# Decode attention: PV with V as the moving operand in four column tiles, the diagonal taken out by masked sums and one fp32 matmul

## The chip, the cores and the metric

The kernel runs on one core of one Trainium2 chip. The metric is the device time of one execution in microseconds. Inputs lie in HBM; the core has five engines with a queue of instructions each: TensorE (PE, with its weight loads as PEld), VectorE (DVE), ScalarE (ACT), GpSimd (POOL) and SyncE (SP), which here issues all DMAs.

## The reference

Two layers of grouped-query decode attention, each followed by a small dense block, for 8 sequences of one token. Every layer reads the same K and V caches: 8 sequences x 8 kv heads x 8192 keys x 128, bf16, K and V 134 MB each. Four query heads share one kv head.

```python
def _A_ref(x, k_cache, v_cache, wq, wo):          # x (8, 1, 512)
    q = (x @ wq).reshape(B, 1, 32, 128).transpose(0, 2, 1, 3)
    k, v = jnp.repeat(k_cache, 4, axis=1), jnp.repeat(v_cache, 4, axis=1)
    scores = jnp.einsum("bhqd,bhkd->bhqk", q, k) * 128 ** -0.5
    o = jnp.einsum("bhqk,bhkd->bhqd", softmax(scores), v)
    return o.transpose(0, 2, 1, 3).reshape(B, 1, 4096) @ wo
def _B_ref(x, w1, w2):                             # 512 -> 1792 -> 512
    return silu(x @ w1) @ w2

x = x + _A_ref(_layernorm(x), k_cache, v_cache, wq, wo)
x = x + _B_ref(_layernorm(x), w1, w2)
x = x + _A_ref(_layernorm(x), k_cache, v_cache, wq, wo)
x = x + _B_ref(_layernorm(x), w1, w2)
```

## The kernel before

**Tasks, positions, granules.** One task is one (layer, sequence, kv head): 128 tasks. A task has 8 positions of 1024 keys (8 chunks of 128); two positions are one granule of 2048 keys, which is one tile of 512 KB of K or V in one slot of the arena (`NSLOT` = 27 slots). `make_tasks` orders the tasks so that the two layers interleave: the transposed K of the last five kv heads of a sequence (20 granules, `KEEP`) stays in the arena from layer 0 to layer 1. So 88 tasks load K and V and transpose K; 40 tasks (layer 1, kept heads) load V only and need no transposes. `plan_loads` sorts all loads by the position that needs them and gives each the slot that comes free first; `issue_until(p)` at the end of each position issues, on SP's queue, the loads whose slot has been given up by then. A DMA waits on the queue for the instructions that still read its slot.

**One loop over positions** (L744) writes all engines' work in order; each engine runs its queue in that order. `op` and `mm_group` put a semaphore wait in front of an instruction where a resource that it reads or writes was last touched by another engine (or by VectorE or ScalarE themselves). At position p the loop does, in this order:
- at p7 (p mod 8 = 7), the four query columns of the next task go into `QB` (ScalarE, L452);
- `emit_t`: 8 transposes of the K chunks into a PSUM bank `TPp` (L429, three banks), then one copy back into the arena over the same chunks: the granule's first half (even p) on ScalarE (L435), the second (odd p) on VectorE (L437);
- at odd p, `emit_pv` twice (L533): the PV matmuls of the granule 12 positions back (`LP`);
- a piece of the softmax of the task before, by p mod 8 (`soft`): p0 row maximum and `spread` (L471, L473); p1 the shift: an fp32 matmul with `ones` (L481), `own`, `shift` (L484, L487) and the exponential on ScalarE (L491), which writes P; p3 the sums (L497, and a reduction over partitions on GpSimd, L500); p4 four transposes of P and the copy to `PT` (L509, L513); p7 the reciprocal;
- if a layer chain is pending, its next stage; else, at some odd p, a group of 16 output-projection matmuls (`add_heads`, L627);
- at odd p, `emit_s` (L460): the scores of the granule, 4 matmuls that stream 512 keys each past 32 query columns into four column tiles of one PSUM bank. They need both halves' copies;
- at p4, for the task whose PV ended at p3, `emit_norm` (L547) on VectorE.

**Scores.** The four column tiles take the four quarters of a granule; granule k of the task shifts the query columns by k within the tile, so that after four granules the bank holds 4 tiles x (4 query heads x 4 granules) rows of 512 scores. After the transposes of P, `PT` holds for each key lane the weights by chunk x (0 to 3 within a quarter), quarter c, head r and granule k.

**PV.** Each of the 64 chunks of V (128 keys x 128) is the stationary operand, and its four weight columns, each repeated 12 times (`PVN`), are the moving one; all 64 matmuls accumulate into one PSUM region of the bank `OTp`, 128 x 48, of which every twelfth column is used. The same bank is also the target of the shift matmul.

**Layer chains.** When the last task of a sequence in layer 0 is normed, a chain of stages follows, one per position: the remaining `add_heads`, the residual, the layer norm (`first` to `fourth`, short VectorE operations with two reductions on GpSimd), the dense block in two pieces each (28 matmuls a piece), `silu`, a layer norm again, and the query projection of layer 1 in 8 pieces. There are eight such chains. The final dense block for all sequences stands at the end.

Of the kernel before, what the change touches and what calls it, by code (L numbers as in the profile page):

```python
# [29 lines left out]
FAR = 1e38  # L30
PVN = 12
CW = 32
# [176 lines left out]
def _build(ctx, nc, A_x, A_k_cache, A_v_cache, A_wq, A_wo, B_w1, B_w2, out):  # L209
# [58 lines left out]
    QT2 = [sb([128, HQ], BF16, "QT2") for _ in range(2)]  # L268
    QB = [sb([128, NGRAN - 1 + QUAD], BF16, "QB") for _ in range(NQB)]
    at1 = [sb([128, HQ], BF16, "at1") for _ in range(3)]  # L270
    at2 = sb([128, HQ, B], BF16, "at2")
    vr = sb([128, B], FP32, "vr")
# [11 lines left out]
    Xr = P  # L284
    PT = [sb([128, CPB, NQ * USED], BF16, "PT") for _ in range(NPT)]
    ones = sb([128, 128], FP32, "ones")
    hm = sb([128, REP], FP32, "hm")
    real = sb([128, 1], FP32, "real")
    far = sb([128, NQ * USED], FP32, "far")
    rowmax = sb([128, 1], FP32, "rowmax")  # L290
# [25 lines left out]
    def r_half(slot, h):  # L316
        return res(f"slot{slot}_{h}")
# [40 lines left out]
    with nc.Block() as block:  # L358

        @block.sync  # L360
        def _(sync_eng):
# [12 lines left out]
            for n in range(NQB):  # L374
# [4 lines left out]
                lambda: dve.tensor_reduce(  # L379
                    hm[:, :], lanes.rearrange("p c (r k) -> p r c k", k=NGRAN), AX.XY, ALU.add),  # L380
                reads=["ident"], writes=["hm"],
            )
            op(dve, lambda: dve.tensor_reduce(real[:, :], hm[:, :], AX.X, ALU.add), reads=["hm"], writes=["real"])
            for c in range(NQ):
                op(dve, lambda c=c: dve.tensor_scalar(
                    far[:, c * USED:(c + 1) * USED].rearrange("p (r k) -> p r k", k=NGRAN),
                    hm[:, :].unsqueeze(2).to_broadcast([128, REP, NGRAN]), real[:, 0:1], -FAR,
                    op0=ALU.subtract, op1=ALU.mult),
                   reads=["hm", "real"], writes=["far"])
# [21 lines left out]
            evacs = [0]  # L411
            tnext = [0]

            def has_t(i):
# [7 lines left out]
            def emit_t(i):  # L422
                b, g, k, h = where(i)
                slot = k_slot[(b, g, k)]
                tb = evacs[0] % NTP
                evacs[0] += 1
                tpv = TPp[tb][:, :].rearrange("p (k q) -> p k q", q=128)
                steps = [
                    lambda c=c: pe.transpose(tpv[:, c, :], chunk(slot, h * GRP + c), ident[:, :])  # L429
                    for c in range(GRP)  # L430
                ]
                mm_group(steps, reads=[r_half(slot, h), "ident"], writes=[f"TP{tb}"])
                dst = half(slot, h)
                if h == 0:
                    op(act, lambda: act.copy(dst, TPp[tb][:, :]), reads=[f"TP{tb}"], writes=[r_half(slot, h)])  # L435
                else:
                    op(dve, lambda: dve.tensor_copy(dst, TPp[tb][:, :]), reads=[f"TP{tb}"], writes=[r_half(slot, h)])  # L437
# [7 lines left out]
            def emit_q(ti):  # L445
                layer, b, g = tasks[ti]
                if layer == 0:
                    q, rq = QT1[:, b * HQ + g * REP:b * HQ + (g + 1) * REP], "QT1"
                else:
                    q, rq = QT2[b % 2][:, g * REP:(g + 1) * REP], f"QT2_{b % 2}"  # L450
                qb = QB[ti % NQB][:, NGRAN - 1:NGRAN - 1 + USED].rearrange("p (r k) -> p r k", k=NGRAN)[:, :, 0]
                op(act, lambda: act.copy(qb, q), reads=[rq], writes=[f"QB{ti % NQB}"])  # L452

            def emit_s(i):
                ti = i // GPT
                b, g, k, _h = where(i)
                slot = k_slot[(b, g, k)]
                bank, qn = ti % NSCP, ti % NQB
                steps = [
                    lambda c=c: pe.matmul(  # L460
                        SCp[bank][c * QUAD:(c + 1) * QUAD, :], QB[qn][:, NGRAN - 1 - k:NGRAN - 1 - k + QUAD],
                        ARENA[:, slot * SLOT + c * KB:slot * SLOT + (c + 1) * KB],
                        start=(k == 0), stop=(k == NGRAN - 1),
                    )
                    for c in range(NQ)
                ]
                mm_group(steps, reads=[r_half(slot, 0), r_half(slot, 1), f"QB{qn}"], writes=[f"SC{bank}"])

# [34 lines left out]
            def emit_pt(ti):  # L503
# [9 lines left out]
                op(dve, lambda: dve.tensor_copy(  # L513
                    PT[pb][:, :, :].rearrange("p x (c q) -> p x c q", q=USED),
                    tpv.rearrange("p x (c q) -> p x c q", q=QUAD)[:, :, :, 0:USED]),
                   reads=[f"TP{tb}"], writes=[f"PT{pb}"])

# [4 lines left out]
            def emit_pv(i):  # L522
                ti = i // GPT
                b, g, k, h = where(i)
                slot = v_slot[(b, g, k)]
                ob, pb = ti % 2, ti % NPT
                pv = PT[pb][:, :, :].rearrange("p x (c r k) -> p x c k r", c=NQ, k=NGRAN)
                otp = OTp[ob][:, 0:REP * PVN].rearrange("p (r n) -> p r n", n=PVN)
                steps = []
                for c in range(GRP):  # L530
                    cc = (i % GPT) * GRP + c
                    steps.append(
                        lambda c=c, cc=cc: pe.matmul(  # L533
                            otp, chunk(slot, h * GRP + c), pv[:, cc % CPB, cc // CPB % NQ, k, :].unsqueeze(2).to_broadcast([128, REP, PVN]),
                            start=(cc == 0), stop=(cc == NCH - 1),
                        )
                    )
                mm_group(steps, reads=[r_half(slot, h), f"PT{pb}"], writes=[f"OT{ob}"])

            def emit_norm(ti):  # L540
# [4 lines left out]
                else:  # L545
                    dst, rd = at2[:, g * REP:(g + 1) * REP, b], "at2"
                op(dve, lambda: dve.tensor_tensor(dst, OTp[ob][:, 0:REP * PVN:PVN], rcp[st][:, :], ALU.mult),  # L547
                   reads=[f"OT{ob}", f"rcp{st}"], writes=[rd])
# [72 lines left out]
            def wo_part(g, rhs_of, r_rhs, n, first, last):  # L621
                w = CW if n == 1 else n
                steps = []
                for o in range(KT):
                    for h in range(g * REP, (g + 1) * REP):
# [7 lines left out]
                        )  # L633
                mm_group(steps, reads=["wo", r_rhs], writes=["MISC"])

# [51 lines left out]
            def query(n, dst_of, rdst, parts=1):  # L687
# [4 lines left out]
                        lambda: dve.tensor_copy(dst_of, MISC[:, 0:HQ * n].rearrange("p (h b) -> p h b", b=n)),  # L692
                        reads=["MISC"], writes=[rdst],
                    ))

            def chain_of(b):
                xs = [XT[n][:, :, b:b + 1] for n in range(3)]
                st = block_stages(xs, ["XT0", "XT1", "XT2"], 1, True)
                st += ln_stages(xs[2], "XT2", 1) + settle
                return st + query(1, QT2[b % 2][:, 0:HQ].rearrange("p (h b) -> p h b", b=1), f"QT2_{b % 2}", QPARTS)  # L700

# [3 lines left out]
            def add_heads(b):  # L705
# [3 lines left out]
                if b < B:  # L709
                    a = at1[b % 3]  # L710
                    wo_part(g, lambda h: a[:, h:h + 1], f"at1_{b % 3}", 1, first, last)
                else:
                    wo_part(g, lambda h: at2[:, h, :], "at2", B, first, last)

# [16 lines left out]
            soft = {0: [softmax_max], 1: [softmax_shift, softmax_exp], 3: [softmax_sum], 4: [emit_pt], 7: [softmax_rcp]}  # L731
            for f in query(B, QT1[:, 0:B * HQ].rearrange("p (b h) -> p h b", h=HQ), "QT1"):
                f()

            emit_q(0)

            chain = []
            chain_b = [None]
# [4 lines left out]

            for p in range(NG + LP + GPT + 1):  # L744
                tq = (p + LQ) // GPT
# [6 lines left out]
                emit_t_until(p + LT)  # L752
                if p % GPG == GPG - 1:
                    for i in range(p - LP - GPG + 1, p - LP + 1):
                        if 0 <= i < NG:
                            emit_pv(i)
                ti, ph = p // GPT - 1, p % GPT
# [3 lines left out]
                if chain:  # L761
                    left = max(1, first1[chain_b[0]] - EARLY - p)
                    late = len(chain) <= QPARTS or len(chain) > left + QPARTS // 2
                    for _n in range(2 if late and len(chain) > left else 1):
                        chain.pop(0)()
                elif heads[turn[0]] and (p >= NG or turn[0] == B
                                         or p % GPG == GPG - 1 and (tasks[p // GPT][2], 0) in kept):
                    add_heads(turn[0])
                if p < NG and p % GPG == GPG - 1:
                    emit_s(p)  # L770
                done = p - LP - GPT
                if done >= 0 and done % GPT == 0 and done // GPT < ntask:
                    tj = done // GPT
                    emit_norm(tj)
                    layer, b, _g = tasks[tj]
                    if layer == 0:
                        heads[b].append(_g)
                    elif b == B - 1:
                        heads[B].append(_g)
                    if layer == 0 and tj == last0[b]:  # L780
                        assert not chain and turn[0] == b
# [52 lines left out]
```

## Time and profile before

| | |
|---|---|
| median of 3 runs | 1204.68 us (1202.18 to 1208.07) |
| profiled execution, its own time | 1209.39 us |
| profiled execution, span from the first to the last instruction | 1207.3 us |
| mean granted TensorE clock | 0.974 |
| HBM read | 465.05 MB |
| DMA rate in the slices of the span | 355 to 410 GB/s, the first and last slices aside |
| busy: PE, PEld, VectorE, ScalarE, GpSimd | 977, 777, 564, 463, 71 us |
| K copies: ScalarE (352), VectorE (352) | 1010 ns, 692 ns each |
| PV matmuls | 8192 |
| score matmuls | 2048 |
| chain that ended last, by engine | PE 50%, DMA 19%, DVE 18%, SP's queue 5%, issue 5%, ACT 3% |

Busy time is the union of an engine's instructions, matmul ends are modelled, and a busy TensorE includes waiting in its pipeline. A timeline row gives the start in us from the span's start, the duration in us, the engine, the line of the kernel, the operation, what it writes and reads, the number of instructions merged in it, and, in brackets, the idle time of the engine before it with the instruction that ended it. A row of a group in the page ends with its busy time, the mean ns of one and the idle time before.

### The profile page before, as it was taken

What the parts mean: (1) busy time and instruction counts of PE and PEld (TensorE: products, weight loads), DVE (VectorE), ACT (ScalarE), POOL (GpSimd) and SP (SyncE); (2) the same over time, 40 slices, a digit from 0 to 9 for tenths busy, and PEclk for the clock granted to TensorE, in tenths of its full rate; (3) what the DMA queues carried; (4) which work ended last, traced back from release to release, by engine and by line L of the source; (5) the groups of instructions that cost most, each with busy time, mean ns of one, the idle gap of its engine ahead of it and who ended that gap; (6) DMA issues with size and microseconds to landing.
All of it is one profiled execution on the core that took longest, in us unless ns stands there. A gap on an engine that the chain in (4) does not pass through costs nothing.

```text
span 1207.3 us, 45534 instructions
## 1 busy us (share of the span) xinstructions
PE 976.7 (81%) x19960; PEld 777.3 (64%) x19960; DVE 563.8 (47%) x1745; ACT 462.5 (38%) x746; POOL 70.9 (6%) x172
## 2 busy tenths in 40 slices
PE   3688887888888888888888888888788888888785
PEld 3566675766667675676666765667576766677564
DVE  2434453545344553455344544445344543445443
ACT  1334341544235431453244432544144422454241
POOL 0000000000000000000000000000000000000000
PEclk9989998999899998999999999999999997999997
DMA  9999999999999999999999999999999999999993
GB/s 370 385 397 407 394 358 403 408 399 385 387 408 407 401 367 409 408 394 388 379 408 406 399 365 408 408 405 362 398 408 406 393 371 409 408 366 377 393 407 155
DMA packets 131622, 468.03 MB, mean 388 GB/s; under 512 B 13904, under 2 KB 19808, under 8 KB 130912
## 3 DMA queue, kind: packets, MB, share of 16 engines
q1 hardware_dynamic: 131424, 465.12, 98.6%
q8 instruction: 158, 2.59, 0.9%
q14 instruction: 40, 0.33, 0.1%
HBM read 465.05 MB, written 0.01 MB: 385 GB/s over the span
## 4 chain that ended last, share of the span: by engine, by line
PE 50%; DMA 19%; DVE 18%; SPq 5%; issue 5%; ACT 3%; POOL 0%; POOLq 0%; ACTq 0%; DVEq 0%
PE TPp L429 19%; PE SCp L460 11%; DVE arena L437 9%; DMA arena<-in_A_v_cache_dram 9%; PE OTp L533 9%; DMA arena<-in_A_k_cache_dram 8%; SPq L333 5%; PE MISC L609 4%; PE TPp L509 3%; DVE rowmax L471 2%; DMA wo<-in_A_wo_dram 2%; PE OTp L481 2%; ACT P L491 2%; PE MISC L627 2%; DVE PT L513 1%
## 5 line engine op out<-in xcount | busy, mean ns | idle before, releaser
L435 ACT COPY arena<-TPp 128x1024 bf16<-128x1024 bf16 x352 | 355.7, 1010 | 437.2 <-PE TPp L429 437.1
L429 PE MATMUL TPp<-ident,arena 128*128 128x128 bf16 x5632 | 403.3, 222 | 25.0 <-DMA arena<-in_A_k_cache_dram 11.0
L429 PEld LDWEIGHTS TPp<-ident,arena 128*128 128x128 bf16 x5632 | 325.3, 99 | 111.3 <-issue 73.2
L437 DVE COPY arena<-TPp 128x1024 bf16<-128x1024 bf16 x352 | 243.3, 692 | 263.0 <-PE TPp L429 256.6
L533 PE MATMUL OTp<-PT,arena 128*128 128x48 bf16 x8192 | 299.8, 185 | 45.4 <-DVE at L547 17.6
L533 PEld LDWEIGHTS OTp<-PT,arena 128*128 128x128 bf16 x8192 | 256.6, 97 | 106.6 <-issue 77.7
L460 PE MATMUL SCp<-arena,QB 128*32 128x512 bf16 x2048 | 211.5, 401 | 97.3 <-DVE ssm L497 32.4
L491 ACT ACTIVATE P<-SCp,shift 128x512 bf16<-128x512 f32 x128 | 88.0, 687 | 279.9 <-PE OTp L533 163.0
L471 DVE TENSOR_REDUCE rowmax<-SCp 128x1 f32<-128x512 f32 x128 | 88.5, 692 | 129.5 <-PE SCp L460 129.5
L460 PEld LDWEIGHTS SCp<-arena,QB 128*32 128x32 bf16 x2048 | 60.3, 94 | 131.4 <-ACT arena L435 45.6
L500 POOL PARTITION_ALL_REDUCE ssa<-ssm x128 | 55.9, 437 | 957.6 <-DVE ssm L497 929.8
L513 DVE COPY PT<-TPp 128x256 bf16<-128x256 bf16 x128 | 37.3, 292 | 112.6 <-PE TPp L509 112.6
L481 PE MATMUL OTp<-spread,ones 128*128 128x64 f32 x256 | 54.6, 295 | 23.6 <-DVE spread L473 22.2
L509 PE MATMUL TPp<-ident,P 128*128 128x128 bf16 x512 | 50.4, 221 | 11.6 <-ACT P L491 11.6
L481 PEld LDWEIGHTS OTp<-spread,ones 128*128 128x128 f32 x256 | 38.7, 191 | 26.8 <-DVE spread L473 26.8
L484 DVE SCALAR_TENSOR_TENSOR own<-OTp,real,far 128x64 f32<-128x64 f32 x128 | 36.3, 284 | 40.3 <-PE OTp L481 40.0
L509 PEld LDWEIGHTS TPp<-ident,P 128*128 128x128 bf16 x512 | 32.6, 98 | 23.5 <-ACT P L491 22.1
L497 DVE TENSOR_SCALAR ssm<-hm,rs 128x4 f32<-128x4 f32 x128 | 28.6, 223 | 36.7 <-ACT P L491 36.7
L627 PE MATMUL MISC<-at,wo 128*128 128x32 bf16 (+1 forms) x1152 | 40.0, 176 | 6.1 <-DMA wo<-in_A_wo_dram 5.9
L609 PE MATMUL MISC<-xnT,wq 128*128 128x32 bf16 (+1 forms) x1152 | 38.7, 176 | 1.9 <-issue 1.9
L627 PEld LDWEIGHTS MISC<-at,wo 128*128 128x128 bf16 x1152 | 35.2, 97 | 6.4 <-DMA wo<-in_A_wo_dram 6.0
L609 PEld LDWEIGHTS MISC<-xnT,wq 128*128 128x128 bf16 x1152 | 35.1, 97 | 3.7 <-issue 3.7
(47 smaller groups left out, 296.3 us busy)
## 6 DMA issues: line engine op xcount, KB each, us to landing
arena<-in_A_v_cache_dram SPq DMA_DIRECT2D x512, 512.0 KB, 9.6
arena<-in_A_k_cache_dram SPq DMA_DIRECT2D x352, 512.0 KB, 14.2
wq<-in_A_wq_dram SPq DMA_DIRECT2D x1, 4096.0 KB, 16.3
wo<-in_A_wo_dram SPq DMA_DIRECT2D x1, 4096.0 KB, 26.0
w<-in_B_w_dram SPq DMA_DIRECT2D x2, 1792.0 KB, 22.6
P<-in_A_x_dram SPq DMA_DIRECT2D x1, 8.0 KB
out_dram<-P SPq DMA_DIRECT2D x1, 8.0 KB
```

The costliest lines, as they stand in the source:

```text
L333: eng.dma_start(out_ap, in_ap).then_inc(counter.sem, 16)
L429: lambda c=c: pe.transpose(tpv[:, c, :], chunk(slot, h * GRP + c), ident[:, :])
L435: op(act, lambda: act.copy(dst, TPp[tb][:, :]), reads=[f"TP{tb}"], writes=[r_half(slot, h)])
L437: op(dve, lambda: dve.tensor_copy(dst, TPp[tb][:, :]), reads=[f"TP{tb}"], writes=[r_half(slot, h)])
L460: lambda c=c: pe.matmul(SCp[bank][c * QUAD:(c + 1) * QUAD, :], QB[qn][:, NGRAN - 1 - k:NGRAN - 1 - k + QUAD], ARENA[:, slot * SLOT + c * K ...
L471: op(dve, lambda: dve.tensor_reduce(rowmax[:, :], SCp[bank][:, :], AX.X, ALU.max), reads=[f"SC{bank}"], writes=["rowmax"])
L481: mm_group([lambda: pe.matmul(every, ones[:, :], spread[:, :], start=True, stop=True)], reads=["ones", "spread"], writes=[f"OT{ob}"])
L491: op(act, lambda: act.activation(P[:, :], SCp[bank][:, :], ACT.Exp, bias=shift[:, 0:1], scale=SM_SCALE, accum_out=rs[st][:, :]), reads=[f" ...
L509: lambda c=c: pe.transpose(tpv[:, c, :], P[:, c * 128:(c + 1) * 128], ident[:, :])
L533: lambda c=c, cc=cc: pe.matmul(otp, chunk(slot, h * GRP + c), pv[:, cc % CPB, cc // CPB % NQ, k, :].unsqueeze(2).to_broadcast([128, REP, P ...
L609: lambda o=o, k=k: pe.matmul(MISC[:, o * n:o * n + w], w_sb[:, k, o * 128:(o + 1) * 128], rhs_of(k).to_broadcast([128, w]) if n == 1 else ...
L627: lambda o=o, h=h: pe.matmul(MISC[:, o * w:(o + 1) * w], wo_sb[:, h, o * 128:(o + 1) * 128], rhs_of(h).to_broadcast([128, w]) if n == 1 el ...
```

## The change

PV changes its operands. The weights of a quarter of a granule (128 x 16: four chunks x by four heads r) become the stationary operand, and a quarter of V (128 x 512, its four chunks side by side) moves past it; the four quarters go into four column tiles of the bank, at partitions 0, 32, 64 and 96, 16 rows each. So a granule has 4 matmuls instead of 16, and four granules accumulate. Of the 16 x 512 results of a tile, only the blocks are wanted in which the weights' chunk and V's chunk are the same, the diagonal. `emit_diag` adds the four column blocks of 128 with a mask per row (`xm`, one column per chunk) into `diag`, 128 x 128 fp32, in four VectorE operations, each on the result of the one before; `emit_pick` then sums rows over chunks and tiles and turns the result, by an fp32 matmul with `diag` stationary and `hm` (128 x 4) moving, into columns 0 to 3 of the same bank. `emit_norm` reads these. The layouts of `QB`, `PT`, `hm` and `far` change their order from (head, granule) to (granule, head) to suit, and `at2` is now `QT1`'s memory.

In the order of work: at odd p, PV is written directly in front of the scores, behind the softmax piece and the chain's stage, instead of directly behind the transposes. The four sums are written at the end of p4, the pick matmul at p5 directly behind the transposes, and the norm at the end of p5 instead of p4; with it the heads and the chain start one position later. In a granule at whose first half the next chain stage is `second`, `third`, `fourth` or `silu`, the two K copies change engine: the first half is copied by VectorE, the second by ScalarE.

```diff
-    QB = [sb([128, NGRAN - 1 + QUAD], BF16, "QB") for _ in range(NQB)]
+    QB = [sb([128, (NGRAN - 1) * REP + QUAD], BF16, "QB") for _ in range(NQB)]
-    at2 = sb([128, HQ, B], BF16, "at2")
+    at2 = QT1
-    PT = [sb([128, CPB, NQ * USED], BF16, "PT") for _ in range(NPT)]
+    PT = [sb([128, NQ, NGRAN, CPB * REP], BF16, "PT") for _ in range(NPT)]
+    xm = sb([128, CPB], FP32, "xm")
+    diag = sb([128, DH], FP32, "diag")
...
+            op(
+                dve,
+                lambda: dve.tensor_reduce(
+                    xm[:, :], lanes.rearrange("p c (x r) -> p x c r", r=REP), AX.XY, ALU.add),
+                reads=["ident"], writes=["xm"],
+            )
+            for n in range(2):
+                op(dve, lambda n=n: dve.memset(OTp[n][:, :], 0.0), writes=[f"OT{n}"])
...
                 if h == 0:
+                    turned[0] = bool(chain) and chain[0].__name__ in ("second", "third", "fourth", "silu")
+                if (h == 0) != turned[0]:
                     op(act, lambda: act.copy(dst, TPp[tb][:, :]), reads=[f"TP{tb}"], writes=[r_half(slot, h)])
                 else:
                     op(dve, lambda: dve.tensor_copy(dst, TPp[tb][:, :]), reads=[f"TP{tb}"], writes=[r_half(slot, h)])
...
                 op(dve, lambda: dve.tensor_copy(
-                    PT[pb][:, :, :].rearrange("p x (c q) -> p x c q", q=USED),
-                    tpv.rearrange("p x (c q) -> p x c q", q=QUAD)[:, :, :, 0:USED]),
+                    PT[pb][:, :, :, :].rearrange("p c k (x r) -> p x c k r", r=REP),
+                    tpv.rearrange("p x (c q) -> p x c q", q=QUAD)[:, :, :, 0:USED].rearrange(
+                        "p x c (k r) -> p x c k r", r=REP)),
                    reads=[f"TP{tb}"], writes=[f"PT{pb}"])
...
-                for c in range(GRP):
-                    cc = (i % GPT) * GRP + c
-                    steps.append(
-                        lambda c=c, cc=cc: pe.matmul(
-                            otp, chunk(slot, h * GRP + c), pv[:, cc % CPB, cc // CPB % NQ, k, :].unsqueeze(2).to_broadcast([128, REP, PVN]),
-                            start=(cc == 0), stop=(cc == NCH - 1),
-                        )
+                steps = [
+                    lambda c=c: pe.matmul(
+                        OTp[ob][c * QUAD:c * QUAD + CPB * REP, :], PT[pb][:, c, k, :],
+                        ARENA[:, slot * SLOT + c * KB:slot * SLOT + (c + 1) * KB],
+                        start=(k == 0), stop=(k == NGRAN - 1),
                     )
-                mm_group(steps, reads=[r_half(slot, h), f"PT{pb}"], writes=[f"OT{ob}"])
+                    for c in range(NQ)
+                ]
+                mm_group(steps, reads=[r_half(slot, 0), r_half(slot, 1), f"PT{pb}"], writes=[f"OT{ob}"])
+
+            def emit_diag(ti):
+                ob = ti % 2
+                for x in range(CPB):
+                    part = OTp[ob][:, x * DH:(x + 1) * DH]
+                    if x == 0:
+                        op(dve, lambda: dve.tensor_scalar(diag[:, :], part, xm[:, 0:1], None, op0=ALU.mult),
+                           reads=[f"OT{ob}", "xm"], writes=["diag"])
+                    else:
+                        op(dve, lambda: dve.scalar_tensor_tensor(
+                            diag[:, :], part, xm[:, x:x + 1], diag[:, :], op0=ALU.mult, op1=ALU.add),
+                           reads=[f"OT{ob}", "xm", "diag"], writes=["diag"])
+
+            def emit_pick(ti):
+                ob = ti % 2
+                mm_group([lambda: pe.matmul(OTp[ob][:, 0:REP], diag[:, :], hm[:, :], start=True, stop=True)],
+                         reads=["diag", "hm"], writes=[f"OT{ob}"])
...
-                op(dve, lambda: dve.tensor_tensor(dst, OTp[ob][:, 0:REP * PVN:PVN], rcp[st][:, :], ALU.mult),
+                op(dve, lambda: dve.tensor_tensor(dst, OTp[ob][:, 0:REP], rcp[st][:, :], ALU.mult),
...
                 emit_t_until(p + LT)
-                if p % GPG == GPG - 1:
-                    for i in range(p - LP - GPG + 1, p - LP + 1):
-                        if 0 <= i < NG:
-                            emit_pv(i)
+                done, late = divmod(p - LP - GPT, GPT)
+                if late == 1 and 0 <= done < ntask:
+                    emit_pick(done)
...
-                if p < NG and p % GPG == GPG - 1:
-                    emit_s(p)
...
+                if p % GPG == GPG - 1:
+                    if 0 <= p - LP < NG:
+                        emit_pv(p - LP)
+                    if p < NG:
+                        emit_s(p)
+                if late == 0 and 0 <= done < ntask:
+                    emit_diag(done)
+                if late == 1 and 0 <= done < ntask:
+                    emit_norm(done)
```

## The prediction

> **What bounds the kernel now.** I name positions by their place in a task, p0 to p7 (p mod 8); two positions make a granule, and the score group (L460, "S") that closes a granule stands at p1, p3, p5 or p7. The views, in order: the page (DMA 387 to 409 GB/s in most slices, no engine over 81%), then the timeline of one task with transposes and of one without, then the waits. The page names the groups whose durations I use.
>
> ```profile
> span 1207.3 us, 45534 instructions
> ...
> L437 DVE COPY arena<-TPp 128x1024 bf16<-128x1024 bf16 x352 | 243.3, 692 | 263.0 <-PE TPp L429 256.6
> ...
> L471 DVE TENSOR_REDUCE rowmax<-SCp 128x1 f32<-128x512 f32 x128 | 88.5, 692 | 129.5 <-PE SCp L460 129.5
> ...
> L484 DVE SCALAR_TENSOR_TENSOR own<-OTp,real,far 128x64 f32<-128x64 f32 x128 | 36.3, 284 | 40.3 <-PE OTp L481 40.0
> ```
>
> The reader sees: VectorE takes 0.692 us for a 512-column fp32 PSUM row and 0.284 us for 64 columns with two tensors and a pointer scalar. Columns cost (692 - 220) / (512 - 64) = 1.05 ns each (220 ns is L487's 64-column reduce), so a short operation is mostly fixed cost.
>
> The timeline of a task with transposes, far from any layer chain:
>
> ```profile
> 483.28 0.40 PE L460 MATMUL SCp<-arena,QB 128*32 128x512 bf16 x4 [0.47 <-DVE ssm L497]
> ...
> 484.07 0.39 PE L509 MATMUL TPp<-ident,P 128*128 128x128 bf16 x4
> ...
> 484.50 0.29 DVE L513 COPY PT<-TPp 128x256 bf16<-128x256 bf16 x1 [1.22 <-PE TPp L509]
> 484.70 0.16 DVE L547 TENSOR_TENSOR at<-OTp,rcp 128x4 bf16<-128x4 f32 x1
> 484.93 0.56 PE L533 MATMUL OTp<-PT,arena 128*128 128x48 bf16 x16
> 484.94 0.69 DVE L437 COPY arena<-TPp 128x1024 bf16<-128x1024 bf16 x1
> ...
> 485.78 0.40 PE L460 MATMUL SCp<-arena,QB 128*32 128x512 bf16 x4 [0.29 <-DVE arena L437]
> ...
> 488.06 0.40 PE L460 MATMUL SCp<-arena,QB 128*32 128x512 bf16 x4 [0.47 <-DVE rcp L520]
> ```
>
> S waits for the copy of the second half of K on VectorE: the copy ends at 484.94 + 0.69 = 485.63 and S starts 0.15 later. PV (L533) is over before that: its 16 matmuls start 25 ns apart (0.41 us, 484.93 to 485.34), and then TensorE stands still. Granules (S to S: 481.01, 483.28, 485.78, 488.06, 490.33) take 2.27, 2.50, 2.28, 2.27; a task takes 9.32 to 9.33. The four 2.3 us are the loop S, transposes, copy, S; the 0.22 more is the transposes of P (L509). A task without transposes (layer 1, kept heads) takes 5.62 (S at 461.45, and at 467.07 four granules later), by VectorE again: S, maximum, spread, L481, exponential, P's transposes, PT, PV.
>
> Which is the slower, this loop or the DMA? The windows of such stretches move 407 to 409 GB/s. A task with transposes loads eight 512 KB tiles, 4.19 MB, 10.28 us at 408; one without, 2.10 MB, 5.14 us. So the loop is faster than the DMA in the first (9.33 against 10.28) and slower in the second; it runs ahead on filled slots and then waits. Over the program: 88 tasks x 9.33 + 40 x 5.62 = 1046 us, of the 1153 us from the first S (32.72) to the last (1185.69). Eight chains of layer work cost some 7 each (three tasks from 279.16 to 314.27 took 35.11 instead of 28.0), 57 in all; what is left, 50, is waiting for loads (such as the 5.9 for wo) and stretches at half clock. Both limits are close, and 1.0 us more per task uses up what the DMA leaves.
>
> **Part 1: PV.** Sixteen matmuls of 48 columns go, four column tiles of 512 come. The nearest rows are S itself: a group that is followed by full-array work holds TensorE 0.33 us (483.28 to the next transposes at 483.62), and the four groups that follow each other directly at the start (16 matmuls, 1.90 us from 32.72, granted clock 0.5) repeat every 0.42 us, 0.21 at full clock. PV now stands directly before S, so it adds 0.21 to 0.33; I take 0.22. TensorE is freed 0.19 us x 512 granules = 97 us. On the path it is worth nothing in a task with transposes: in each granule S waits for the copy 0.2 to 0.6 us after PV, and this wait grows by what PV saves. In tasks without, two of the four granules (0.84 us: 464.38, 465.21) are TensorE alone and fall to 0.43 to 0.55. PV now comes behind the transposes, the shift matmul and the chain's piece. At p1 the shift matmul L481 loses its cover and waits for spread some 0.1 us (spread ends at 489.48, the transposes at 489.3); in tasks with transposes the copy (to 490.18) still ends last.
>
> **Part 2: the diagonal sums.** At p4, behind the PT copy and before the copy of the second half of K that p5 issues, VectorE gets four operations of 128x128 fp32 from PSUM with a pointer scalar, each waiting for the one before. The price: L484's 284 ns plus 64 columns x 1.05 = 351 ns each for the three with two tensors; L473's 254 plus 67 = 321 for the first; gaps of 30 ns between dependent operations (294.10 + 0.28 to 294.42). Sum 0.32 + 3 x 0.38 = 1.46 us. Bounds: from L487's 220 + 67 = 287 each, 1.24; by doubling L484 with its fixed part, 568 each, 2.36. I take 1.46, as L484 is the same operation.
>
> Shift by shift in the granule above (S at p3 = 0): PT copy 1.22 to 1.51, sums to 2.94, K copy to 3.6, S at 3.75 instead of 2.50: **1.25 us more per task with transposes**. TensorE meanwhile waits at the new fp32 matmul (below) for the sums, from 1.46 to 3.0. That VectorE work ahead of this copy is paid one for one, the chain shows already: seven small operations stand before it here, and S comes 3.34 us after the last (296.96) instead of 2.50.
>
> ```profile
> 298.17 0.29 DVE L513 COPY PT<-TPp 128x256 bf16<-128x256 bf16 x1 [0.73 <-PE TPp L509]
> 298.38 0.14 DVE L577 TENSOR_SCALAR vr<-s1a 128x1 f32<-128x1 f32 x1
> ...
> 299.47 0.68 DVE L437 COPY arena<-TPp 128x1024 bf16<-128x1024 bf16 x1
> ...
> 300.30 0.40 PE L460 MATMUL SCp<-arena,QB 128*32 128x512 bf16 x4 [1.13 <-DVE tr L588]
> ```
>
> In a task without transposes there is no copy, but TensorE's queue holds PV and S behind the new matmul. S at p7 = 0: L481 at 1.5, its PV now behind it (S at p1 0.2 later, off the path), P's transposes at 3.4, PT 3.85 to 4.14, sums to 5.57, pick to 5.9, PV and S to 6.2, the last granule 0.43: 6.6 against 5.62, **1.0 us more**.
>
> [...]
>
> **Part 3: pick and norm.** One fp32 matmul of 4 columns: L481 (fp32, 64 columns) occupies 0.25 us until the next group (293.65 to 293.90). It lies under the K copy where there are transposes and is in the 6.6 where not. The norm moves to p5's end, behind the matmul; at, wo's heads and the chain start one position later.
>
> **Part 4: layouts.** PT is written in runs of 4 instead of 16: between 0.29 (L513) and 1.27 us (the L692 cast of 256 elements with scattered writes). I take 0.29, since runs of 4 are nearer to L513 than single scattered elements; the upper end would put 0.98 on each task. QB grows from 35 to 44 columns, cleared once; hm and far keep their sizes; xm and the two clears of OT are VectorE work before the first S, which waits for loads and wq. at2 lies in QT1, with strided reads in the final projection alone (128 matmuls, 4.4 us). Loads and their slots are the same; a V slot is freed at most 0.5 us later in its granule, under a queue that is 10 to 14 us deep (median from issue to landing).
>
> **Part 5: turned copies.** In a chain's granule with second, third, fourth or silu next, the first half goes to VectorE before the stage and the second to ScalarE (1.01 us instead of 0.69). Such a granule has 2.27 + 0.32 = 2.6 instead of up to 3.38 (291.30 to 294.68 and the like): minus 0.7 in about three granules. But fourth (seven operations, 1.3 us) falls between PT and the sums once a chain: plus 1.7; second likewise plus 0.7. Net nothing (bounds minus 3 and plus 3 per chain, 24 us).
>
> **Sum.** 88 x 1.25 + 40 x 0.98 = 149 us. The loop then needs 10.58 per task, more than the DMA's 10.28, so of the 50 us of waiting I keep 15 (wo, clock): minus 35. 1207.3 + 149 - 35 = 1321 span; the profiled execution's own time is 1209.39, 2.1 over its span and 4.7 over the median 1204.68. Against the median: 1321 + 2.1 - 4.7, **1320 us**.
>
> **Rivals.**
> *A, TensorE's queue is the bound* (ends faster). Price: PV's 97 us, and more where transposes follow at once. What is left is then the DMA: 465.12 MB at 408 GB/s is 1140, plus 8 before the first load and 20 after the last: 1168. For it: TensorE is busy 81%, and in the chain's granules (2.78: 302.82 to 305.60) it has no gap. Against: outside them, L460 waits for a copy in every granule. It decides if S starts straight behind PV. [...]
> *B, the sums are short and the DMA hides them*: if an operation costs 0.22 whatever its columns (L497), the sums take 0.97, a task 10.1, still under 10.28. What shows is 40 tasks x 0.5 and 8 chains x 2 us over 1205, less some 6 of waiting: 1235.
> *C, the PT copy in runs of 4 costs 1.27*: 1320 + 128 x 0.98 = 1445.
>
> **Chances.** Forecast 0.78, A 0.05, B 0.10, C 0.07. The forecast's own spread: sums at 1.24 give 1293, a chain gain of 24 less again 1270; sums at 2.36 give 1320 + 115. Range 1250 to 1400. A measurement tells 0.5% (6 us) from no change: faster 0.05, same 0.02, slower 0.93.
>
> **What would show it.** The sums at 0.32 to 0.35 us, 512 of them; the fp32 matmul's weights waiting for VectorE about 1.5 us per task; S to S at p5 about 3.75 and elsewhere 2.27; tasks without transposes at 6.6; DMA near 350 GB/s evenly, no longer 408. TensorE's busy time falls by more than 60 us while the span grows. I am wrong if the p5 granule stays under 3 us, if the sums take under 0.2, or if DMA stays at 408 in the long stretches.

## The result, and the profile after

| | before | changed | ratio |
|---|---|---|---|
| median | 1206.38 us (4 runs) | 1408.3 us (4 runs, 1402.47 to 1409.81) | 1.166 (95%: 1.160 to 1.172) |
| profiled execution, own time; span | 1209.39; 1207.3 | 1408.25; 1406.5 | |
| mean granted TensorE clock | 0.974 | 0.853 | |
| 87 tasks with transposes, p7 to p7 (the first task left out) | 910.7 | 1013.8 | |
| 40 tasks without | 241.0 | 331.3 | |
| TensorE busy; VectorE busy | 977; 564 | 1014; 719 | |

The change made the kernel 17% slower; the forecast was 1320, with a range from 1250 to 1400. The page after the change (busy, mean ns of one, idle before; the clock in tenths):

```profile
PEclk7899977999599967999599977999599977999676
...
L565 PE MATMUL OTp<-hm,diag 128*128 128x4 f32 x256 | 56.9, 293 | 208.9 <-DVE diag L559 191.3
...
L559 DVE SCALAR_TENSOR_TENSOR diag<-OTp,xm,diag 128x128 f32<-128x128 f32 x384 | 134.7, 351 | 13.6
...
L526 DVE COPY PT<-TPp 128x256 bf16<-128x256 bf16 x128 | 37.1, 290 | 114.9 <-PE TPp L522 114.9
...
L556 DVE TENSOR_SCALAR diag<-OTp,xm 128x128 f32<-128x128 f32 x128 | 43.6, 341 | 2.2 <-PE OTp L542 2.2
```

The reader is to see three things. The four sums cost what was forecast: 341 + 3 x 351 ns, 178 us of VectorE in all. TensorE waits for them, 191 us in front of L565. And the row of clocks, which had nines almost throughout before, now falls to between 5 and 7 at regular places. Before, the row was:

```profile
PEclk9989998999899998999999999999999997999997
```

A mean of 0.853 with 0.5 as the only other value in the trace is (1 - 0.853) x 1406.5 / 0.5 = 413 us at half clock, against 63 before (from the mean of 0.974).

A task with transposes, from the timeline after (start, duration, engine, line, what; in brackets the idle time before), beside the task shown in the prediction:

```profile
411.19 0.40 PE L473 MATMUL SCp<-arena,QB 128*32 128x512 bf16 x4 [0.55 <-DVE ssm L510]
...
412.40 0.29 DVE L526 COPY PT<-TPp 128x256 bf16<-128x256 bf16 x1 [1.22 <-PE TPp L522]
412.61 0.34 DVE L556 TENSOR_SCALAR diag<-OTp,xm 128x128 f32<-128x128 f32 x1
412.99 1.12 DVE L559 SCALAR_TENSOR_TENSOR diag<-OTp,xm,diag 128x128 f32<-128x128 f32 x3
414.03 0.68 DVE L450 COPY arena<-TPp 128x1024 bf16<-128x1024 bf16 x1
414.17 0.39 PE L565 MATMUL OTp<-hm,diag 128*128 128x4 f32 x2 [1.35 <-DVE diag L559]
...
414.85 0.40 PE L473 MATMUL SCp<-arena,QB 128*32 128x512 bf16 x4
```

PT, the sums, then the K copy, then S: 3.66 us from S to S where it was 2.50. The other granules keep their 2.27 (406.64 to 408.92, 408.92 to 411.19). The first sum starts while the second half's transposes still run (412.20 to 412.81), so it hardly lengthens the path; the other three do. The whole task takes 10.49 us, in 41 of the 87; the forecast said 10.58.

A task without transposes, from the timeline before (granted clock 1.00 over its 5.62 us) and from the one after:

```profile
461.45 0.40 PE L460 MATMUL SCp<-arena,QB 128*32 128x512 bf16 x4
...
463.01 0.40 PE L509 MATMUL TPp<-ident,P 128*128 128x128 bf16 x4 [0.33 <-ACT P L491]
...
463.45 0.29 DVE L513 COPY PT<-TPp 128x256 bf16<-128x256 bf16 x1 [0.23 <-PE TPp L509]
...
467.07 0.40 PE L460 MATMUL SCp<-arena,QB 128*32 128x512 bf16 x4
```

```profile
518.26 0.64 PE L473 MATMUL SCp<-arena,QB 128*32 128x512 bf16 x4
...
519.99 0.69 PE L494 MATMUL OTp<-spread,ones 128*128 128x64 f32 x2 [1.09 <-DVE spread L486]
...
522.42 0.61 PE L522 MATMUL TPp<-ident,P 128*128 128x128 bf16 x4
...
523.07 0.29 DVE L526 COPY PT<-TPp 128x256 bf16<-128x256 bf16 x1 [0.69 <-PE TPp L522]
523.28 0.34 DVE L556 TENSOR_SCALAR diag<-OTp,xm 128x128 f32<-128x128 f32 x1
523.65 1.12 DVE L559 SCALAR_TENSOR_TENSOR diag<-OTp,xm,diag 128x128 f32<-128x128 f32 x3
524.83 0.59 PE L565 MATMUL OTp<-hm,diag 128*128 128x4 f32 x2 [1.80 <-DVE diag L559]
525.35 0.60 PE L542 MATMUL OTp<-arena,PT 128*16 128x512 bf16 x4
...
525.74 0.64 PE L473 MATMUL SCp<-arena,QB 128*32 128x512 bf16 x4
...
526.59 0.64 PE L473 MATMUL SCp<-arena,QB 128*32 128x512 bf16 x4
```

From S at p7 to the next S at p7 it takes 8.33 us after the change; the forecast said 6.6. VectorE's rows are as forecast. What is longer is TensorE's: the P transposes take 0.65 us to the copy's start where they took 0.44 (463.01 to 463.45 before), the pick is followed by PV after 0.52 instead of the 0.31 of the task with transposes above (414.17 to 414.48), and a PV and an S hold the engine 0.42 to 0.43 each, twice the 0.21. That is half clock, as the windows of such a stretch say (span, then busy time and instructions of the five engines, clock, DMA share, GB/s):

```profile
510.00:540.00 30.00, 19.93 (x150) 7.85 (x142) 12.52 (x43) 3.44 (x12) 1.72 (x4) 0.50 1.03 408
```

The DMA moves 408 GB/s in these stretches, since they fill the slots that come free, and 199 to 409 in the windows of 30 us of the rest, the last aside; the forecast of an even rate was wrong.

### The profile page after: what moved, and what is told of

It is laid out like the page before. It is cut to its first block, busy times and chain, and to the rows that moved or that the text cites. A ratio compares the mean times of both kernels' runs of the same rounds, so it can differ in the third digit from the quotient of the medians.

```text
span 1406.5 us, 34114 instructions
## 1 busy us (share of the span) xinstructions
PE 1013.9 (72%) x14072; PEld 659.3 (47%) x14072; DVE 719.2 (51%) x2260; ACT 464.0 (33%) x746; POOL 70.2 (5%) x172
## 4 chain that ended last, share of the span: by engine, by line
PE 55%; DVE 34%; DMA 5%; issue 4%; SPq 2%; ACT 0%; POOL 0%; POOLq 0%; ACTq 0%; DVEq 0%
PE TPp L440 17%; PE SCp L473 13%; DVE diag L559 10%; PE OTp L542 9%; DVE arena L450 8%; DVE rowmax L484 5%; PE OTp L565 4%; PE OTp L494 4%; PE MISC L637 3%; DMA arena<-in_A_k_cache_dram 3%; PE TPp L522 3%; DVE PT L526 2%; SPq L334 2%; DVE diag L556 2%; DVE spread L486 2%
## 5 line engine op out<-in xcount | busy, mean ns | idle before, releaser
L440 PE MATMUL TPp<-ident,arena 128*128 128x128 bf16 x5632 | 419.8, 227 | 16.5 <-DVE arena L450 13.8
L440 PEld LDWEIGHTS TPp<-ident,arena 128*128 128x128 bf16 x5632 | 339.0, 101 | 115.8 <-issue 112.0
L473 PE MATMUL SCp<-arena,QB 128*32 128x512 bf16 x2048 | 241.9, 462 | 82.0 <-DVE ssm L510 39.9
L542 PE MATMUL OTp<-arena,PT 128*16 128x512 bf16 x2048 | 236.5, 454 | 2.4 <-DMA arena<-in_A_v_cache_dram 1.8
L565 PE MATMUL OTp<-hm,diag 128*128 128x4 f32 x256 | 56.9, 293 | 208.9 <-DVE diag L559 191.3
L565 PEld LDWEIGHTS OTp<-hm,diag 128*128 128x128 f32 x256 | 45.7, 224 | 235.0 <-DVE diag L559 216.1
L559 DVE SCALAR_TENSOR_TENSOR diag<-OTp,xm,diag 128x128 f32<-128x128 f32 x384 | 134.7, 351 | 13.6
L494 PE MATMUL OTp<-spread,ones 128*128 128x64 f32 x256 | 65.5, 345 | 59.5 <-DVE spread L486 54.4
L542 PEld LDWEIGHTS OTp<-arena,PT 128*16 128x16 bf16 x2048 | 51.7, 92 | 46.9 <-issue 17.1
L497 DVE SCALAR_TENSOR_TENSOR own<-OTp,real,far 128x64 f32<-128x64 f32 x128 | 35.6, 278 | 29.8 <-PE OTp L494 29.8
L556 DVE TENSOR_SCALAR diag<-OTp,xm 128x128 f32<-128x128 f32 x128 | 43.6, 341 | 2.2 <-PE OTp L542 2.2
```

The source lines that it names most:

```text
L473: lambda c=c: pe.matmul(SCp[bank][c * QUAD:(c + 1) * QUAD, :], QB[qn][:, USED - (k + 1) * REP:USED - (k + 1) * REP + QUAD], ARENA[:, slot ...
L494: mm_group([lambda: pe.matmul(every, ones[:, :], spread[:, :], start=True, stop=True)], reads=["ones", "spread"], writes=[f"OT{ob}"])
L542: lambda c=c: pe.matmul(OTp[ob][c * QUAD:c * QUAD + CPB * REP, :], PT[pb][:, c, k, :], ARENA[:, slot * SLOT + c * KB:slot * SLOT + (c + 1) ...
L556: op(dve, lambda: dve.tensor_scalar(diag[:, :], part, xm[:, 0:1], None, op0=ALU.mult), reads=[f"OT{ob}", "xm"], writes=["diag"])
L559: op(dve, lambda: dve.scalar_tensor_tensor(diag[:, :], part, xm[:, x:x + 1], diag[:, :], op0=ALU.mult, op1=ALU.add), reads=[f"OT{ob}", "xm ...
L565: mm_group([lambda: pe.matmul(OTp[ob][:, 0:REP], diag[:, :], hm[:, :], start=True, stop=True)], reads=["diag", "hm"], writes=[f"OT{ob}"])
```

## The experiments

Three explanations had to be told apart for the 8.33 us. *Gate*: TensorE works a smaller share of such a task, since it waits for VectorE, and the granted clock falls. Rivals: *tiles* (the clock falls because the work is narrow column tiles) and *loads* (the tasks wait for V). The runs a1, a2, c1 and d2 are one execution each, the others medians of 4 to 12; executions of the kernel before lie between 1197.65 and 1216.27 us, so a difference of under 20 us from a single execution says little.

**Fillers on TensorE** (a1). Transposes of the identity into a bank that is not in use, in front of the three waits of a task without transposes.

```diff
...
+            def fill(p, n):
+                if p >= NG or has_t(p):
+                    return
+                tb = evacs[0] % NTP
+                mm_group(
+                    [lambda: pe.transpose(TPp[tb][:, 0:128], ident[:, :], ident[:, :])] * n,
+                    reads=["ident"], writes=[f"TP{tb}"])
...
                 emit_t_until(p + LT)
+                if p % GPT in {1: 16, 4: 8, 5: 24}:
+                    fill(p, {1: 16, 4: 8, 5: 24}[p % GPT])
```

> The changed kernel, with filler transposes of the identity into an unused bank at the three places where TensorE stands still in a task without transposes (16 at p1, 8 at p4, 24 at p5, in front of the wait). Theory 'gate' (TensorE stands still for the sums for more than half of such a task, so the granted clock falls to a half there and the task takes 8.33 us instead of the 6.6 of full clock): with the fillers the clock in these stretches is 0.9 or more, the task takes 6.6 to 6.9 and the whole 1335 to 1355 us. Rival 'tiles' (the clock falls because most of the work there is narrow column tiles): clock stays near 0.5, the fillers run at half speed and cost, 1400 to 1440. Rival 'loads' (8.33 us is waiting for V): nothing changes, 1400 to 1415.

Measured: 1349.86 us, 58 less than the changed kernel, with 1920 matmuls more. The 40 tasks take 274.6 instead of 331.3 (57 less); 26 of them 6.57 or 6.58. The tasks with transposes take 1013.8 as in the changed kernel. Its timeline and the window of three such tasks:

```profile
353.38 0.39 PE L481 MATMUL SCp<-arena,QB 128*32 128x512 bf16 x4
...
356.78 0.40 PE L530 MATMUL TPp<-ident,P 128*128 128x128 bf16 x4
357.02 1.50 PE L463 MATMUL TPp<-ident 128*128 128x128 bf16 x24
...
357.43 0.34 DVE L564 TENSOR_SCALAR diag<-OTp,xm 128x128 f32<-128x128 f32 x1
357.80 1.12 DVE L567 SCALAR_TENSOR_TENSOR diag<-OTp,xm,diag 128x128 f32<-128x128 f32 x3
358.98 0.39 PE L573 MATMUL OTp<-hm,diag 128*128 128x4 f32 x2 [0.46 <-DVE diag L567]
...
359.94 0.39 PE L481 MATMUL SCp<-arena,QB 128*32 128x512 bf16 x4
```

```profile
346.80:366.52 19.72, 18.07 (x270) 12.46 (x264) 10.58 (x36) 2.58 (x9) 1.29 (x3) 1.00 1.02 410
```

The same VectorE chain, with full clock on TensorE: 6.56 from S to S, the 6.6 of the forecast. From the PT copy to the pick it is 1.76 us in both (357.22 to 358.98 here, 523.07 to 524.83 there), and the whole difference lies in TensorE's steps. *Loads* falls: in the changed kernel TensorE waits 1.8 us for V in the whole run. *Gate* holds; *tiles* is not excluded by this run alone, since the fillers are full-array work too.

**The sums in the kernel before** (c1). The four sums behind the norm and the pick matmul at p5 in a part of the bank that PV doesn't use, results unused; PV stays in 16 full-array matmuls.

```diff
...
                 emit_t_until(p + LT)
+                prev, late1 = divmod(p - LP - GPT - 1, GPT)
+                if late1 == 0 and 0 <= prev < ntask:
+                    emit_pick(prev)
...
                     emit_norm(tj)
+                    emit_diag(tj)
```

> The kernel before with the four sums at the end of p4 and the pick matmul at p5 added, their result unused; PV stays in 16 full-array matmuls. Theory 'sums on the path': tasks with transposes at 10.5 to 10.6; those without 7.1 at full clock; 1350 to 1400 in all. Theory 'gate' adds: TensorE now idles near half of a task without transposes, and the granted clock in these stretches falls well under the 0.9 of before, the tasks take 7.1 to 8.5. Rival 'tiles': the clock in them stays at 0.9 or more, since PV is full-array work here, and the tasks take 7.1.

Measured: 1451.82 us, 52 above the expected range. Without PV's change the sums and the pick cost 243 us (1208.36 before, beside it); the changed kernel, with all its parts, is 44 faster than this. Tasks with transposes take 10.6 as expected where TensorE has nothing else to do, but 11.0 to 11.4 in 35 of the 87: in most of these a group of 16 output-projection matmuls stands between the pick and S, and the p5 granule takes 4.17 instead of 3.78. Those without take 9.13 in 18 cases, more than the expected 7.1 to 8.5, and 352.5 together. The window of three of them (9.13, 8.39 and 9.13):

```profile
364.13:390.78 26.65, 19.63 (x267) 12.81 (x265) 10.30 (x36) 2.60 (x9) 1.29 (x3) 0.56 1.03 410
```

The clock is 0.56 with full-array PV. Only the scores are in column tiles here, as they were before the change, when the clock in these tasks was 0.935 in the mean. *Tiles* falls as the explanation: the clock goes down without PV's tiles as soon as the sums hold TensorE up.

**One sum of four** (a2; three of the four diagonal blocks are left out of the result).

```diff
-                for x in range(CPB):
+                for x in range(1):
```

> The changed kernel with one of the four sums; three of the four diagonal blocks are left out of the result. Theory 'sums on the path' (the K copy and the pick stand behind them): 3 x 0.38 = 1.12 us less in each task: tasks with transposes at 9.4 again and partly waiting for loads again, those without 1.1 less (7.2 at half clock); together 88 x 0.9 + 40 x 1.1, so 1275 to 1300 us. Rival 'the layout or PV tiles cost it': within 20 us of 1408.

Measured: 1282.02 us, 126 less; tasks with transposes back at 9.33 in 34 cases, those without at 7.18 in most (1.15 less, at a clock of 0.54). Each of the three sums left out was paid in full by the granule that waited for it; the one that is left costs the p5 granule next to nothing (2.51 against 2.50), since the copy behind it has to wait for its transposes anyway. That the gain is smaller than three sums in each task with transposes (927.4 together, not 1013.8 - 87 x 1.12 = 916) goes with the waiting for loads that comes back: TensorE waits 21.4 us for K, V and wo here, 4.1 in the changed kernel.

**The sums moved behind the K copy** (b1): the sums at p5 after the copy, the pick at the next p0.

```diff
...
-                if late == 1 and 0 <= done < ntask:
+                if late == 1 and 0 <= done < ntask:
+                    emit_diag(done)
+                if late == 4 and 0 <= done < ntask:
                     emit_pick(done)
...
-                if late == 0 and 0 <= done < ntask:
-                    emit_diag(done)
-                if late == 1 and 0 <= done < ntask:
+                if late == 4 and 0 <= done < ntask:
                     emit_norm(done)
```

> The changed kernel with the four sums behind the K copy of p5 instead of in front of it, the pick matmul at the next p0 and the norm behind it: nothing waits for the sums. Theory 'sums on the path': tasks with transposes back to 9.33 (p5 granule 2.5), those without 5.2 at full clock. Theory 'gate': TensorE does only some 2.4 us of work in such a task, the clock is still at a half in many of them and they take 6 to 7: 1195 to 1250 us in all. Rival 'tiles': the same clock, the same time. Rival 'no gate, sums alone': clock 0.95 or more, 1175 to 1195.

Measured: 1241.15 us, 1.0254 of before (1.0207 to 1.0301). The p5 granule is 2.50 again at best. The pick now stands between the two groups of transposes of p0 and p1 and costs 0.2 there (9.52 in such tasks). The tasks without take 4.99 to 5.18 at full clock and 6.55 at half; both occur, often within one stretch, and the clock over the 40 is 0.75 in the mean. Of the kernel's loss, 35 us lie in the 24 tasks that the eight layer chains fall in (316.4 instead of 281.8); the other tasks with transposes take together what they took before.

**The turned copies alone** (a3): `turned[0] = False`.

> The changed kernel without the change of engine of the two K copies beside long VectorE stages. The prediction had this part at nothing (3 us per chain either way, 24 in all). If it gains (the K copy no longer stands behind a VectorE stage): 1415 to 1435 us without it. If it costs (a ScalarE copy is 0.32 us longer and ends the granule): 1385 to 1400. If neither: within 7 us of 1408.

Measured: 1391.45 us, ratio to before 1.151 (1.1449 to 1.1571; the changed kernel's 1.166 had 1.160 to 1.172): the turned copies cost 17 us. Three tasks around a chain took 13.74 + 15.72 + 12.46 = 41.9 with them and 12.43 + 13.51 + 12.25 = 38.2 without (31.5 without any chain). One granule of each, S to S, first the changed kernel, then this one:

```profile
1095.82 0.40 PE L473 MATMUL SCp<-arena,QB 128*32 128x512 bf16 x4
...
1097.25 1.01 ACT L448 COPY arena<-TPp 128x1024 bf16<-128x1024 bf16 x1 [0.32 <-PE TPp L440]
...
1098.41 0.40 PE L473 MATMUL SCp<-arena,QB 128*32 128x512 bf16 x4 [0.87 <-ACT arena L448]
```

```profile
1082.72 0.40 PE L473 MATMUL SCp<-arena,QB 128*32 128x512 bf16 x4
...
1084.15 0.69 DVE L450 COPY arena<-TPp 128x1024 bf16<-128x1024 bf16 x1
...
1084.99 0.40 PE L473 MATMUL SCp<-arena,QB 128*32 128x512 bf16 x4 [0.55 <-DVE ssm L510]
```

The ScalarE copy of the second half runs 1.01 us where VectorE takes 0.69, so S comes after 2.59 instead of 2.27. What it was to save, a K copy held up by a stage, is nothing in this granule: without the turn, the stage (`second`, 1083.61 to 1084.17) is over when the second half's transposes are.

**Both terms** (d2): the fillers of a1 with `turned[0] = False`; no other edit.

> The changed kernel with both the fillers and without the change of engine of the K copies. If the two terms add (58 us for the clock, 17 for the copies): 1330 to 1338 us. If the copies cost only at half clock: 1345 to 1352.

Measured: 1326.61 us, 82 below the changed kernel and 3 under the expected range: the two add (58 and 17); the 7 beyond that are within the spread of single executions.

**Sums off the path and fillers** (b2), and the same without the turn (b3). As b1, but the pick at p7 behind the transposes where the position has any; fillers 14, 8 and 8.

```diff
...
+                at = 3 if p - late + 3 < NG and has_t(p - late + 3) else 4
+                if late == at and 0 <= done < ntask:
                     emit_pick(done)
...
```

> The changed kernel with the four sums behind the K copy of p5, the pick matmul at p7 behind the transposes where there are any (at the next p0 where not) and the norm behind it, and fillers on TensorE in tasks without transposes (14 at p1, 8 at p4, 8 at p5). If the two causes, the sums on the path and the half clock, are all: tasks with transposes 9.33 at best, those without 5.2 to 5.4 at a clock over 0.9, together 1185 to 1215 us, the chains' granules being what is left over. If the clock doesn't follow TensorE's work: 1230 to 1245 like the variant without fillers.

> The same as the last one without the change of engine of the K copies in the chains. If the turn gains there: 10 to 25 us above the last one; if it costs: 5 to 20 below; else within 6.

Measured: b2 1220.78 us, 1.0076 of before (1.0044 to 1.0107); b3 1231.53, 1.0179 (1.0135 to 1.0223). Here the turn gains 11. The tasks without transposes take 211.4, 30 less than before the change, at full clock throughout. The tasks with transposes take 946.6, 36 more. Of these, 16 lie in the 24 tasks around the chains; three of them take 11.99 + 12.73 + 13.33 = 38.1 against 34.5 before the change, and in the timeline of one chain the sums stand in front of its VectorE stages (963.31 to 964.8, then `third`, then the K copy at 965.75). The other 20 lie away from the chains, where 40 of the tasks take 10.1 to 10.3, about the 10.28 that the DMA needs: TensorE waits 39.6 us for K, 11.0 before. Most of what the tasks without transposes gain is so given back as waiting for loads. The expected 1185 to 1215 was missed by 6 us; another order at the chains was not tried.

**Fillers in the kernel before** (d1): 8, 6 and 9 at p1, p4 and p5, PV and all else as before.

> The kernel before with filler transposes on TensorE in tasks without transposes (8 at p1, 6 at p4, 9 at p5, each in front of a wait that is at least as long), nothing else. Before, the clock in these tasks averages 0.935 and they take 6.02 us in the mean, 5.62 at best. If the clock is what the 0.4 are: 5.7 in the mean and up to 13 us less of TensorE's loop, of which the DMA leaves part: 1195 to 1205 beside a before of 1207 to 1211. If the wait for V is: no change.

Measured: 1200.88 us, 0.9947 of before (0.992 to 0.9973): by 0.5% the one version that is faster than the kernel before. The clock in the 40 tasks is 1.00 instead of 0.935; they take 237.6 instead of 241.0, less of a gain than expected: 19 take the 5.62, where 15 did, but in two others the p5 granule takes 3.21 and 3.58 instead of 2.40 and 2.09, the second with a pause of 1.0 us inside PV that the trace puts down to nothing, and in a dozen more it takes 0.1 to 0.5 longer. The cause of the pause stays open.

## Why the prediction was wrong

- *What bounds the kernel.* Right: a loop through the K copy, close to the DMA's limit. One sum of four brings the 9.33 back, and moving all four behind the copy nearly does (9.52, with the pick between the transposes).
- *Part 2, tasks with transposes.* Right: 1.16 us more per task (10.49 against 9.33), forecast 1.25; the p5 granule 3.66, forecast 3.75.
- *Part 2, tasks without transposes.* **The step that failed.** "6.6 against 5.62, 1.0 us more" prices L481, P's transposes, the pick, PV and S at full clock. At full clock that sum holds, and so do nearly all of its times (a1: L502, the shift, 1.47 after S, P's transposes 3.40, the PT copy 3.84, the pick 5.60, S 6.56). As it ran it measures 8.33, at a granted clock of 0.50. Left out was what the longer waits for the sums do to TensorE's clock: it fell to half, and the term 40 x 0.98 should have been 40 x 2.3 (331.3 - 241.0 = 90). That is 58 of the 88 us between 1320 and 1408, shown by a1. The prediction had the half clock in "15 (wo, clock)" as a remainder of the kernel before and took it to stay as it was. Its upper price for the sums would have given 1435, beyond its own range of 1400; that the measured time lies under this price would be luck, since the sums cost what was forecast.
- *Part 5.* "Net nothing" was mis-sized: minus 17 us for taking the turn out (a3). The sign is not fixed: it gains 11 where the sums are off the path (b2 against b3).
- *Sum.* With fillers and without the turn the kernel runs 1326.6 (d2, one execution), 7 from the forecast. The waiting for loads did go, as "minus 35" had it: TensorE's waits for K, V and wo fell from 29.8 to 4.1 us. An even DMA rate near 350 GB/s did not come: it stays at 408 to 410 in the tasks without transposes.
- *Part 1 and the order.* The 0.21 us of a group in tiles at full clock holds (a1, 355.22 to 355.87 in three steps, clock 1.00). The trace of before has no clock record at 32.72; in the changed kernel the same 16 matmuls take 1.90 us from 34.84, at a recorded 0.50. TensorE time saved by PV is worth nothing in a task with transposes, as said (2.27 stays). In the others it is worth 26 us in sum once nothing waits for the sums and the clock is full (211.4 in b2 against 237.6 in d1); by the commonest task, 5.15 against 5.62, it is 19. "TensorE's busy time falls by more than 60" was wrong: it rose from 977 to 1014. PV's own fell, from 300 to 237, but the pick added 57, which the sentence left out, and the scores (212 to 242), the transposes of K (403 to 420) and the shift (55 to 66) lasted longer, in part at half clock.
- *Part 4.* Right: PT costs 290 ns in runs of 4 (292 before). Rival C is out, and so are A (TensorE's queue: S still waits for the copy) and B (short sums: they take 341 and 351 ns).

## What to carry to other kernels

Price a stretch that waits more with the clock that such waiting brought: here 2.4 us of work in 6.6 at full clock, with a pause of 1.8, went with 0.50 to 0.56 behind the first task of a stretch, and 5.1 in 6.57, with a pause of 0.5, with 1.00. Add up the engine's work, divide by the new length, look at the longest pause, and compare both with stretches of the same trace where the clock stayed. A few columns more on VectorE are dear where a copy behind them ends the loop (four sums of 128 columns, 341 and 351 ns each, cost 1.16 us a task); the place in the queue, not the busy share, decided here: the same four sums behind the copy instead of in front of it, with the pick and the norm later, were worth 167 us (1408 to 1241). Work that frees an engine which is not the last to finish buys nothing (the 2.27 stayed), and may take from it the load that kept its clock up: in b1, where nothing waits for the sums, the clock in the 40 tasks is 0.75 where it was 0.935.

## What the runs showed of the hardware

The clock fell where TensorE stood still more. In a stretch of the changed kernel (343 to 385 us) TensorE stands still for at most 1.8 us at a time, and the clock is 0.50 over four whole tasks on end (351.26 to 384.60). The work in a task is an estimate, from the groups' own spacing at full clock: PV and S 0.21 each in tiles (a1, 355.22 to 355.87), the shift 0.25 (before, 293.65 to 293.90), P's transposes 0.22 (d1, 581.92 to 582.14), the pick 0.25 (0.20 in b1, 245.76 to 245.96, and 0.31 in the changed kernel, 414.17 to 414.48), a filler 0.056 (a1, 1.07 for 16 and 0.62 for 8). Beside it stand the length of a task at full clock (for the changed kernel that of a1; for c1 an estimate, 5.62 with 1.55 for the sums, 523.28 to 524.83 above, and 0.31 for the pick), the longest pause that the traces show in such tasks, and the mean clock over the 40:

| | work, us | share | longest pause, us | mean clock |
|---|---|---|---|---|
| a1 (48 fillers) | 5.1 of 6.57 | 78% | 0.5 | 1.00 |
| before (5.62 less the waits of 0.74, 0.40 and 0.64, by spacing) | 3.84 of 5.62 | 68% | 0.6 (0.8 in one) | 0.935 |
| c1 (the 3.84 and the pick) | 4.1 of 7.5 | 55% | 1.9 | 0.64 |
| b1 | 2.4 of 5.0 | 48% | 0.8 | 0.75 |
| changed | 2.4 of 6.6 | 36% | 1.8 | 0.59 |

In these runs less work and longer pauses go with a lower clock. Which of the two the clock follows they don't separate: c1 has a larger share than b1, longer pauses, and the lower clock. In the changed kernel, at 36%, the clock falls to 0.56 or less in all but the first task of each stretch. In its trace the half clock comes in pieces of 3.41 us and multiples of it, up to 40.96; the only other value is full clock.
